# Splitting one Strassen-Winograd product once more, and planning the order anew

## The chip, the cores and the metric

The kernel runs on one core of one Trainium2 chip. The metric is the device time of one execution in microseconds (us), the median of several. TensorE (PE) multiplies matrices, VectorE (DVE), ScalarE (ACT) and GpSimd (POOL) work elementwise, SyncE (SP) issues DMAs.

## The reference

Two parts follow each other. The first is a linear attention with a decaying state (RWKV 5) for batch 4, 8 heads, 768 steps and head size 48:

```python
for t in range(S):
    kt, vt, rt = (k[:, :, t].copy(), v[:, :, t].copy(), r[:, :, t].copy())
    cur = np.einsum('bhd,bhe->bhde', u[None] * kt, vt)
    y[:, :, t] = np.einsum('bhd,bhde->bhe', rt, state + cur)
    state = w[None, :, :, None] * state + np.einsum('bhd,bhe->bhde', kt, vt)
```

Its output, as 3072 tokens of 384 features, goes through a mixture of four experts with hidden size 1024, weighted by the normalised `domain_probs`:

```python
p = domain_probs / (domain_probs.sum(-1, keepdims=True) + 1e-09)
for e in range(E):
    h = np.maximum(x @ w1[e], 0.0)
    out += p[:, e:e + 1] * (h @ w2[e])
```

## The kernel before

The 3072 tokens are 24 chunks of 128 tokens; chunk `ci` is piece `ci // 4` of batch `ci % 4`. Four chunks, one of each batch, make a superchunk; there are six (0 to 5). Each chunk goes through attention: scaling of K and R by powers of the decay (L392, L397), transposes (on PE, or by DMA from chunk 8 on, L442), the products At (L509), a mask (L523, L526), the product Y (L549, L556), the addition of the direct term `dv` (L571) and the new state (L629, L638, L648). GpSimd makes `ruk` and `dv` (L409, L417, L435).

A superchunk then goes through the experts. In superchunks 0 and 1 the second layer is an ordinary product (L738), scaled by the expert's probability on the way out (L749). From superchunk 2 on (`SCALED = 2`) the probability is multiplied in ahead of the first layer (L591), so that the second layer becomes one long product over all four experts: hidden activations of all experts (4096 values of each token, in `hAll`) times `w2` (4096 x 384). First comes the hidden layer of the four experts (`moe`, L707, with the relu L718), 32 groups of three matmuls of 512 columns; then the product stage.

The product stage uses the Strassen-Winograd scheme. For a pair of chunks (`q` = 0 or 1 within the superchunk), A has two block rows (the two chunks) and two block columns (even and odd blocks of 128 hidden values), B = `w2` has two block rows and two block columns of `DH` = 192 output columns. Seven products M1 to M7 replace eight; each is 16 matmuls of 192 columns, in two halves `hf` (experts 0 and 1, experts 2 and 3) of eight matmuls. M1 and M2 are A11 B11 and A12 B21 and meet in the first columns of the first chunk. The sums of A's blocks are made on VectorE (`sum_job`, L874): sum 1 goes into a buffer of its own, sums 3, 2 and 4 are written over blocks of A. The sums of B's blocks are made once (`mix`, L818). M6, M5 and M3 are added onto M1's PSUM region and M4 onto M7's (`ONTO`), each after the copy (ScalarE, L932) or the addition (VectorE, L934) of what stood there before: these are the jobs `C`. The last product of all is M3 of the last pair: its result leaves in two halves, through `o_last` (L927, DMA from SP) and through a ScalarE copy (L929, DMA from ScalarE's queue). The other rows are stored from SP (`store`, L785).

The order of work on each engine is computed when the kernel is built: every piece is a `job` with an estimated duration on each engine, what it needs, a rank, and the buffers that it takes and drops. A list scheduler runs through simulated time, starts on each free engine the ready job with the lowest rank, and the resulting order is issued as it stands. PE's order in the product stage is written out by hand (`SEQ_P`), as is the order of the loads on SP (`ORDER`). `GATES` holds back the scaling of each pair of chunks from chunk 8 on until a given piece of the experts' work is done. After 85 us of simulated time (`LATE`) durations are lengthened: `SLOWER` multiplies those of some engines, and `SHARED` lengthens VectorE's SBUF operations by a share of the time that GpSimd's current operation still takes:

```python
if e == "V" and now > LATE and j.name[0] in ("sum", "scale", "mix", "Xs"):
    us += SHARED * min(us, max(0.0, avail["P"] - now))
```

Of the kernel before, what the change touches and what calls it, by code (L numbers as in the profile page):

```python
# [9 lines left out]
F32 = mybir.dt.float32  # L10
BF16 = mybir.dt.bfloat16
# [3 lines left out]
ALU = mybir.AluOpType  # L15
# [4 lines left out]
def kernel(  # L20
# [12 lines left out]
    nc = tc.nc  # L33

    B, H, S, D = r.shape
    HD = H * D
    C = 128
    NCH = S // C
    TOTC = B * NCH
    SUB = B  # L40
# [81 lines left out]
    for b in range(B):  # L122
# [14 lines left out]

    GATES = [3, 5, 8, 8, 16, 17, 7, 23]  # L140
    WARM, NSPIN = 6.6, 6
    TAIL = {"T": 0.27, "V": 0.17, "A": 0.20, "P": 0.17, "S": 0.0}
    DMAT = 8
# [6 lines left out]
    FIRST = 2  # L150
    SCALED = 2
    ONTO = {6: 1, 5: 6, 3: 5, 4: 7}
    MIX_RANK = 16.0
    XS_ON = {'A': 0.61}
    MIX_ON = {'V': 0.97}
    SCALE_US = 0.97
    VB_ON = {'A': 0.42, 'P': 0.5}
    XS_RANK = 0
    SUM_RANK = -60
    EARLY_SUM = 0.0  # L160
    NSH = 4
    SEQ_S = (((1, 0), (3, 0), (2, 0), (1, 1), (3, 1), (2, 1), (4, 0), (4, 1)),
             ((1, 2), (3, 2), (2, 2), (4, 2)))
    LATE, SLOWER = 85.0, {"V": 1.13, "P": 1.06, "A": 1.15}
    SHARED = 0.6
    SLOTS += [(e, sc, 0) for sc in range(2, SCALED) for e in range(E)]
    ORDER_P = (1, 2, 6, 7, 4, 5, 3)
    SEQ_P = ((0, 1, 0), (0, 2, 0), (0, 7, 0), (0, 1, 1), (0, 2, 1), (0, 7, 1), (0, 6, 0), (0, 6, 1), (0, 4, 0),
# [1 line left out]
             (1, 7, 0), (1, 7, 1), (1, 6, 0), (1, 6, 1), (1, 4, 0), (1, 5, 0), (1, 5, 1), (1, 4, 1), (1, 3, 0),  # L170
             (1, 3, 1))
    EARLY_P = 6
    slots = dict(inp=NIN, wst=NST, RKT=4, AtM=2, Ysb=3, ruk=3, dv=3, Vb=4, At=2, tr=1, ys=1,
                 mm=4, xTe=3, hTs=3, oacc=6, Yse0=1, Yse1=1, Tn=2)
    slots.update({f"{n}{i}": 1 for n, m in (("xTs", 2), ("h", 4), ("S", NSH)) for i in range(m)})
# [6 lines left out]
    def job(name, on, run, needs=(), rank=0.0, takes=(), drops=(), moves=None,  # L182
            behind=()):
        j = Job()
        j.behind = behind
        j.name, j.on, j.run, j.needs, j.rank = name, on, run, list(needs), rank
        j.takes, j.drops, j.moves = takes, drops, moves
        for k in drops:
            tokens[k] = tokens.get(k, 0) + 1
        j.pad = 0.0  # L190
        ci = name[1] if isinstance(name, tuple) and name[0] in ATT else -1
        if ci >= SUB:

            j.pad = PAD_PE if "T" in on else PAD
        j.no = len(jobs)
        assert name not in jobs
        jobs[name] = j
# [61 lines left out]
    def load_p():  # L259
# [1 line left out]
            prow, moe_domain_probs.rearrange("(n p) e -> n p e", p=C)))  # L261

    ORDER = ("K0 K1 R0 R2 R1 V0 K2 w1e0.1 w1e0.0 w1e0.2 V1 K3 V2 R3 w2e0.0 V3 w2e0.1 w2e0.2 p K4 w1e1.1 "
             "w1e1.0 R4 w2e1.0 w1e1.2 K5 R5 w2e1.1 w2e1.2 w1e2.1 V4 w1e2.2 w1e2.0 V5 w2e2.2 V7 K7 w2e2.1 "
             "V6 K6 V8 R6 R7 w2e2.0 w1e3.2 w1e3.1 w1e3.0 K8 V10 K10 w2e3.0 V11 R8 K9 R11 R9 R10 V9 w2e3.2 "
             "K11 V13 w2e3.1 K13 R12 V12 K12 R13 " +
             " ".join(f"c{i}" for i in range(14, TOTC))).split()
    for what in ORDER:
        if what == "p":
            load_p()  # L270
# [93 lines left out]
    def attention(ci):  # L364
# [288 lines left out]
        if c == 0:  # L653
            job(("S", ci), {"V": 0.56}, sv, [("Sm", ci), ("Yout", SUB - 1)], rk + 2, (), (("ys", "S", ci),))
        else:
            job(("Sv", ci), {"V": 0.5}, sv, [("Sm", ci)], rk - 0.1, (("Tn", ci),), (("ys", "S", ci),))
            job(("S", ci), {"P": 1.3}, sp, [("Sv", ci)], rk - 0.5, (), (("Tn", ci),))

    y_sb = weights.tile([128, 3 * HD], BF16)
    y_free, y_at = [0, 1, 2], {}  # L660
# [9 lines left out]
    def h_tag(e, sc):  # L670
        return f"h{3 - e}" if sc >= SCALED else "hTs"
# [170 lines left out]

    s_no, s_last = [0], [None]

    def products(sc, q, at0):
        of = {(m, hf): at0 + n / 7 for n, (x, m, hf) in enumerate(SEQ_P) if x == q}
        c1, c2 = sc * SUB + 2 * q, sc * SUB + 2 * q + 1
        s1, s2 = 2 * q, 2 * q + 1

# [5 lines left out]
        relus = [[("relu", e, sc, fb, 0) for e in (2 * hf, 2 * hf + 1) for fb in range(NFB)]  # L855
                 for hf in range(2)]
        hts = [tuple((h_tag(e, sc), e, sc) for e in (2 * hf, 2 * hf + 1)) for hf in range(2)]
        at_of = {m: of[m, 0] for m in ORDER_P}
        no = s_no[0] % (NSH // 2) * 2
        s_no[0] += 1  # L860
        s_tok = [(f"S{no + hf}", sc, q) for hf in range(2)]
# [5 lines left out]
        def sum_job(k, hf):  # L867
            hs = (0, 1) if hf == 2 else (hf,)

            def run():  # L870
                o, x, y, op = {1: (None, A21, A22, ALU.subtract), 3: (A21, A21, A11, ALU.subtract),
                               2: (A11, None, A11, ALU.subtract), 4: (A12, A12, A11, ALU.add)}[k]
                o, x, y = (s1_of(hf) if z is None else a_of(z, hf) for z in (o, x, y))
                nc.vector.tensor_tensor(o, x, y, op=op)  # L874
            needs = all_cast + [n for h in hs for n in relus[h]]
            if k == 3 and q:
                needs.append(("C", sc, 0, 5))
            if k in (2, 4):
                needs += [("P", sc, q, 1 if k == 2 else 2, h) for h in hs]
            job(("sum", sc, q, k, hf), {"V": 1.23 if hf == 2 else 0.7}, run, needs,  # L880
                at_of[{1: 6, 3: 6, 2: 6, 4: 3}[k]] + (EARLY_SUM if k in (1, 3) and not q and not hf else SUM_RANK), tuple(s_tok[h] for h in hs) if k == 1 else (),
                tuple(x for h in hs for x in hts[h]) + (tuple(s_tok[h] for h in hs) if k in (1, 2) else ()),
                behind=(s_last[0],) if s_last[0] else ())
            s_last[0] = ("sum", sc, q, k, hf)
            for h in hs:
                sum_at[k, h] = s_last[0]
        sum_at = {}
        for k, hf in SEQ_S[q]:
            sum_job(k, hf)
        SUM_OF = {6: 2, 7: 3, 5: 1, 3: 4}  # L890
        def product(m, hf):
# [22 lines left out]
                behind=(p_last[0],) if p_last[0] else ())  # L914
            p_last[0] = ("P", sc, q, m, hf)

        for m in ORDER_P:
            at = at_of[m]

            def c_job(m, s, h, first, drop=()):  # L920
                def run():
                    oacc(c1)
                    o = tl["oacc", c1 // 2][:, s, h * DH:(h + 1) * DH]
                    ps = tl["P", sc, q, m]
                    if m == 3 and c2 == TOTC - 1:
                        rows = out[row0(c1):row0(c1) + C, DH:Dm]
                        nc.vector.tensor_copy(o_last, ps[:, DH // 2:DH])  # L927
                        nc.sync.dma_start(rows[:, DH // 2:DH], o_last)
                        nc.scalar.copy(o[:, 0:DH // 2], ps[:, 0:DH // 2])  # L929
                        nc.scalar.dma_start(rows[:, 0:DH // 2], o[:, 0:DH // 2])  # L930
                    elif first:
                        nc.scalar.copy(o, ps)  # L932
                    else:
                        nc.vector.tensor_add(o, o, ps)  # L934
                needs = [("P", sc, q, m, 1)] + ([] if first else [("C", sc, q, {2: 1, 5: 7, 4: 6}[m])])
                job(("C", sc, q, m), {"A": 0.3} if first else {"V": 0.33}, run, needs, at - 90,
                    (("oacc", c1 // 2),) if m == 1 else (), tuple(("mm", "P", sc, q, x) for x in drop))
            if m == 1:
                c_job(1, 0, 0, True)
            elif m == 2:  # L940
                c_job(2, 0, 0, False, (2,))
                if c2 == TOTC - 1:
                    store(c1, [("C", sc, q, 2)], 0, DH)
            elif m == 6:
                c_job(6, 1, 0, True)
            elif m == 7:
                c_job(7, 1, 1, True)
            elif m == 5:
                c_job(5, 1, 1, False)
            elif m == 4:  # L950
                c_job(4, 1, 0, False, (7,))
                store(c2, [("C", sc, q, 4), ("C", sc, q, 5)])
            else:
                c_job(3, 0, 1, True, (1,))
                if c2 != TOTC - 1:
                    store(c1, [("C", sc, q, 3), ("C", sc, q, 2)])
        return product

    for k, (e, sc, single) in enumerate(SLOTS):
        moe(k, e, sc, single)  # L960
# [22 lines left out]
    for sc in range(SCALED, NSC):  # L983
        at = 8 * (sc - SCALED) + len(SLOTS)
        for e in range(E):
            moe(at + e, e, sc, 0)
        if sc < FIRST:
            for s in range(SUB):
                summed(sc, s, 10.0 + at + 4 + s)
        else:  # L990
            of_pair = [products(sc, q, 10.0 + at + 4) for q in range(2)]
            for q, m, hf in SEQ_P:
                of_pair[q](m, hf)


    left = {j.name: {n for n in j.needs} for j in jobs.values()}
# [33 lines left out]
    events = []  # L1030
    started = []
    gone = set()
    unknown = {n: len(q) for n, q in left.items()}
    known = {n: 0.0 for n in left}
    soon = {e: [] for e in avail}
# [18 lines left out]
    def start(e):  # L1054
# [31 lines left out]
                held.add(t)  # L1086
                free[t[0]] -= 1
        us = j.on[e] * (2.0 if e == "T" and now < WARM and j.name not in ("wmm", "umm") else 1.0)
        if e in SLOWER and now > LATE and j.name[0] not in ("sum", "Xs", "mix", "scale"):
            us *= SLOWER[e]  # L1090
        if e == "V" and now > LATE and j.name[0] in ("sum", "scale", "mix", "Xs"):
            us += SHARED * min(us, max(0.0, avail["P"] - now))
        if j.moves:
            taken, end = dma(now, us, *j.moves)
            us = taken - now + 0.04
        started.append((now, len(started), e, j))
        avail[e] = now + us
        if not j.moves:
            end = now + us + TAIL[e]
        heapq.heappush(events, (avail[e], seq, "eng", e))  # L1100
        heapq.heappush(events, (end, seq + 1, "done", j))
        for u2 in users.get(j.name, ()):
# [8 lines left out]
    while n_done < len(jobs):  # L1111
# [4 lines left out]
            _, _, what, x = heapq.heappop(events)  # L1116
            batch.append((what, x))
        for what, x in batch:
            if what == "done":
                n_done += 1  # L1120
                for t in x.drops:
                    count[t] -= 1
# [63 lines left out]
```

## Time and profile before

| | |
|---|---|
| time, median of 3 runs | 287.18 us (287.02 to 287.48) |
| profiled execution, first to last instruction (span) | 285.2 us |
| time of the profiled execution outside its span | not given by the page; the median is 2.0 us over the span |
| PE busy | 279.3 us, 2677 matmuls |
| VectorE / ScalarE / GpSimd busy | 179.8 / 186.5 / 105.1 us |
| granted TensorE clock | 1.000 |
| DMA, mean | 149 GB/s |

Rows of the profile name a line of the kernel, the engine, the operation, what it writes and reads, the shape, and how often. A matmul's end is modelled, so a matmul's duration is no measure of the rate; the spacing of starts is. The column "idle before" tells what ended the engine's wait. The chain of waits is followed back from the last instruction.

### The profile page before, as it was taken

The numbers are of one execution on the slowest core, as the hardware profiler recorded it, in microseconds if no ns is written. First come the engines' busy times: TensorE is split into PE (matmuls) and PEld (weight loads), VectorE is DVE, ScalarE is ACT, GpSimd is POOL, SyncE is SP. The second block draws the span as 40 slices with busy tenths as digits, with TensorE's granted clock in tenths as the row PEclk, the third lists the DMA queues.
The fourth block names the chain that finished last, engine by engine and source line by source line (L and its number), as shares of the span: only waits on it lengthen the run. The fifth ranks groups of instructions, "written<-read, shape, count | busy, mean of one in ns | idle before, by whom it ended". The sixth has DMA issues, their size and how long they took to land.

```text
span 285.2 us, 6681 instructions
## 1 busy us (share of the span) xinstructions
PE 279.3 (98%) x2677; PEld 193.1 (68%) x2677; DVE 179.8 (63%) x289; ACT 186.5 (65%) x344; POOL 105.1 (37%) x126
## 2 busy tenths in 40 slices
PE   8989999999999999999999999999999999999995
PEld 3777555965774656445899545899644799444995
DVE  5867976679649675998687547798433473010761
ACT  3776868754747485788657788853699850899110
POOL 2883343662796655026157253667010000000000
PEclk9999999999999999999999999999999999999999
DMA  7999999899994988895474996798821241100011
GB/s 152 281 249 339 250 317 268 221 275 238 229 169 91 172 191 143 212 198 118 81 142 116 185 202 118 90 186 129 136 56 28 57 99 42 57 0 0 2 69 44
DMA packets 130290, 42.43 MB, mean 149 GB/s; under 512 B 118458, under 2 KB 130236, under 8 KB 130260
## 3 DMA queue, kind: packets, MB, share of 16 engines
q1 hardware_dynamic: 130100, 41.96, 67.6%
q8 instruction: 21, 0.34, 0.5%
q14 instruction: 9, 0.07, 0.1%
q10 hardware_dynamic: 160, 0.05, 0.1%
HBM read 26.79 MB, written 4.72 MB: 110 GB/s over the span
## 4 chain that ended last, share of the span: by engine, by line
PE 89%; DVE 3%; SPq 3%; DMA 3%; issue 1%; POOL 0%; ACT 0%; DVEq 0%; ACTq 0%
PE hT_ps L707 36%; PE M_ps L905 25%; PE out_ps L738 15%; PE hT_ps L701 5%; DMA RKin<-in_k_dram 3%; SPq L232 2%; PE Y_ps L556 1%; PE At_all L509 1%; PE St_ps L629 1%; PE Y_ps L549 1%; DVE RK_sb L397 1%; PE RKT_ps L461 1%; DVE AtM L523 1%; SPq L246 1%; PE At_ps L509 1%
## 5 line engine op out<-in xcount | busy, mean ns | idle before, releaser
L718 ACT ACTIVATE hAll<-hT_ps 128x512 bf16<-128x512 f32 x168 | 98.7, 597 | 22.5 <-PE hT_ps L707 16.6
L707 PE MATMUL hT_ps<-stg,w_sb 128*128 128x512 bf16 x384 | 85.9, 379 | 0.0
L707 PEld LDWEIGHTS <-w_sb 128*128 128x128 bf16 x504 | 47.2, 98 | 52.2 <-DVE w_sb L80 0.3
L905 PEld LDWEIGHTS <-hAll 128*128 128x128 bf16 x768 | 63.1, 98 | 0.9 <-DVE hAll L874 0.3
L738 PE MATMUL out_ps<-w_sb,hAll 128*128 128x384 bf16 x256 | 45.9, 326 | 0.0
L409 POOL TENSOR_TENSOR ruk<-RKin 128x384 f32<-128x384 f32 x24 | 25.7, 1072 | 50.6 <-DMA RKin<-in_k_dram 31.2
L591 ACT ACTIVATE stg<-dv,p_nat 128x384 bf16<-128x384 f32 x64 | 36.3, 608 | 5.7 <-DMA stg<-stg 5.4
L905 PE MATMUL M_ps<-w_sb,hAll 128*128 128x192 bf16 x384 | 35.3, 246 | 0.0
L932 ACT COPY o_sb<-M_ps 128x192 f32<-128x192 f32 x31 | 9.8, 316 | 37.9 <-PE M_ps L905 37.0
L738 PEld LDWEIGHTS <-hAll 128*128 128x128 bf16 x256 | 23.9, 98 | 15.0
L435 POOL TENSOR_TENSOR dv<-Vt,dcoef 128x384 f32<-128x384 f32 x24 | 21.7, 907 | 27.3 <-ACT stg L591 24.5
L707 PE MATMUL hT_ps<-xTe,w_sb 128*128 128x512 bf16 x120 | 29.2, 379 | 0.0
L417 POOL TENSOR_TENSOR ruk<-ruk,U_sd 128x384 f32<-128x384 f32 x23 | 26.3, 1143 | 1.3
L648 POOL TENSOR_TENSOR S<-Tn,wC 64x192 bf16<-64x192 f32 x32 | 21.6, 674 | 8.2 <-DVE Tn L638 5.1
L874 DVE TENSOR_TENSOR hAll<-stg,hAll 128x1024 bf16<-128x1024 bf16 (+1 forms) x12 | 11.2, 933 | 20.0 <-PE M_ps L905 19.4
L749 DVE SCALAR_TENSOR_TENSOR o_sb<-out_ps,p_nat,o_sb 128x384 f32<-128x384 f32 x24 | 14.7, 616 | 14.0 <-PE out_ps L738 13.3
L874 DVE TENSOR_TENSOR hAll<-hAll 128x1024 bf16<-128x1024 bf16 (+1 forms) x24 | 22.6, 956 | 0.2
L874 DVE TENSOR_TENSOR stg<-hAll 128x1024 bf16<-128x1024 bf16 (+1 forms) x12 | 11.6, 963 | 11.9 <-ACT hAll L718 11.9
L701 PE MATMUL hT_ps<-xTe,w_sb 128*128 128x128 bf16 x288 | 18.7, 219 | 0.0
L934 DVE TENSOR_TENSOR o_sb<-o_sb,M_ps 128x192 f32<-128x192 f32 x24 | 8.4, 351 | 16.3 <-issue 10.3
L905 PE MATMUL M_ps<-w_mix,hAll 128*128 128x192 bf16 x192 | 18.6, 246 | 0.0
L526 DVE TENSOR_TENSOR AtM<-At_all,mask 128x1024 bf16<-128x1024 f32 x8 | 9.7, 1218 | 13.5 <-PE At_all L509 13.5
(89 smaller groups left out, 322.3 us busy)
## 6 DMA issues: line engine op xcount, KB each, us to landing
stg<-in_moe_w_dram SPq DMA_DIRECT2D x16, 576.0 KB, 6.4
RKin<-in_k_dram SPq DMA_DIRECT2D x24, 192.0 KB, 4.3
RKin<-in_r_dram SPq DMA_DIRECT2D x24, 192.0 KB, 3.7
Vt<-in_v_dram SPq DMA_DIRECT2D x24, 192.0 KB, 4.6
out_dram<-o_sb SPq DMA_DIRECT2D x23, 192.0 KB, 2.0
stg<-in_moe_w_dram SPq DMA_DIRECT2D x8, 384.0 KB, 6.4
stg<-stg SPq DMA_TRANSPOSE x32, 2.8
RKT<-RK_sb SPq DMA_TRANSPOSE x16, 3.7
```

The source lines that it names most:

```text
L409: nc.gpsimd.tensor_mul(tl["ruk", ci], tl["Rt", ci], tl["Kt", ci])
L417: nc.gpsimd.tensor_mul(tl["ruk", ci], tl["ruk", ci], U_sd)
L435: nc.gpsimd.tensor_mul(tl["dv", ci], tl["Vt", ci], tl["dcoef", ci].to_broadcast((128, H, D)))
L591: nc.scalar.mul(o, tl["Ysb", ci], p_nat[:, e, n_p:n_p + 1])
L648: nc.gpsimd.tensor_mul(S_new[pr, :, cl], Tn2[pr, tn_at[ci], :, cl], wC[pr, :, None].to_broadcast((P2, NP, D)))
L701: nc.tensor.matmul(ps[:, i, :], w1_sb[:, e, db, (fb + i) * 128:(fb + i + 1) * 128], xTe[:, db, s0, :], start=(i == 0 and db == 0), stop=(i ...
L707: nc.tensor.matmul(ps[:, 0:n, :].rearrange("p a b -> p (a b)"), w1_sb[:, e, db, fb * 128:(fb + 1) * 128], xTe[:, x0 + db, s0:s0 + n, :].re ...
L718: nc.scalar.activation(hTs[:, fb, s0:s0 + n, :], ps[:, 0:n, :], AF.Relu)
L738: nc.tensor.matmul(ps, relu_tile(e, sc)[:, fb, s, :], w2_sb[:, e, fb, :], start=(fb == 0), stop=(fb == NFB - 1))
L749: nc.vector.scalar_tensor_tensor(oacc(ci), in0=tl["o", e, ci], scalar=pe, in1=oacc(ci), op0=ALU.mult, op1=ALU.add)
L874: nc.vector.tensor_tensor(o, x, y, op=op)
L905: nc.tensor.matmul(tl["P", sc, q, m], st, moving(m, hf, n), start=(hf == 0 and n == 0 and m not in ONTO), stop=(hf == 1 and n == 7), skip_ ...
```

## The change

In superchunks 4 and 5 the product M2 is taken out of the seven of each pair. The blocks A12 of both pairs are laid on top of each other and treated as one product, (two block rows: pair 0 and pair 1) x (two block columns) times B21, itself cut into two block rows and two block columns of `DQ` = 96. This product is made with seven products of 96 columns, eight matmuls each (`level2`, jobs `P2`). Its sums of A blocks are the jobs `sum2` (four sums, each in two halves of 512 elements per partition), its sums of B blocks the jobs `mix2` (made once, after the last chunk's attention, in buffers of the K/R loads), and its results are added onto the output rows by jobs `D`, 96 columns at a time. The sums use the `RKT` buffers of attention, the results the PSUM regions `tr` and `ys`. In these superchunks M3's sum (sum 4) also waits for what reads A12 there, all sums of the first level are made in halves, their strict order (`behind`) is dropped, and the PE order is written out as `SEQ_4` and `SEQ_5`; M3 of pair 0 stands next to last there.

The planner now lets a GpSimd operation and a VectorE operation of the kinds in `ONE_PORT` lengthen each other while they overlap; `C` and `D` count as done 0.15 us sooner. The gates, several ranks and the order of the loads after w2e1.2 are others.

```diff
-    GATES = [3, 5, 8, 8, 16, 17, 7, 23]
+    GATES = [4, 3, 8, 8, 15, 11, 20, 18]
...
-    MIX_RANK = 16.0
+    MIX_RANK = 28.0
...
-    XS_RANK = 0
-    SUM_RANK = -60
+    XS_RANK = 2.75
+    SUM_RANK = -50.75
...
-    LATE, SLOWER = 85.0, {"V": 1.13, "P": 1.06, "A": 1.15}
-    SHARED = 0.6
+    LATE, SLOWER = 85.0, {"V": 1.13, "A": 1.15}
+    SHARED = {"V": 0.4, "P": 0.5}
...
+    SEQ_S2 = tuple((k, hf) for k in (1, 3, 2, 4) for hf in range(2))
+    SEQ_4 = ((0, 1, 0), (0, 7, 0), (1, 1, 0), (0, 1, 1), (1, 7, 0), (1, 1, 1), (0, 7, 1), (0, 6, 0), (2, 2, 1),
+             (0, 6, 1), (1, 7, 1), (2, 2, 2), (1, 6, 0), (0, 4, 0), (1, 4, 0), (0, 4, 1), (2, 2, 7), (2, 2, 6),
+             (0, 5, 0), (1, 6, 1), (2, 2, 4), (0, 5, 1), (1, 5, 0), (1, 5, 1), (1, 4, 1), (2, 2, 5), (0, 3, 0),
+             (0, 3, 1), (2, 2, 3), (1, 3, 0), (1, 3, 1))
+    SEQ_5 = ((0, 1, 0), (1, 1, 0), (0, 7, 0), (0, 1, 1), (2, 2, 2), (1, 1, 1), (0, 6, 0), (0, 6, 1), (1, 7, 0),
+             (2, 2, 1), (0, 7, 1), (2, 2, 7), (0, 5, 0), (0, 5, 1), (1, 6, 0), (2, 2, 4), (0, 4, 0), (1, 6, 1),
+             (0, 4, 1), (1, 7, 1), (2, 2, 6), (0, 3, 0), (1, 5, 0), (1, 5, 1), (1, 4, 0), (2, 2, 5), (1, 3, 0),
+             (1, 4, 1), (2, 2, 3), (0, 3, 1), (1, 3, 1))
...
-             "w1e1.0 R4 w2e1.0 w1e1.2 K5 R5 w2e1.1 w2e1.2 w1e2.1 V4 w1e2.2 w1e2.0 V5 w2e2.2 V7 K7 w2e2.1 "
-             "V6 K6 V8 R6 R7 w2e2.0 w1e3.2 w1e3.1 w1e3.0 K8 V10 K10 w2e3.0 V11 R8 K9 R11 R9 R10 V9 w2e3.2 "
-             "K11 V13 w2e3.1 K13 R12 V12 K12 R13 " +
-             " ".join(f"c{i}" for i in range(14, TOTC))).split()
+             "w1e1.0 R4 w2e1.0 w1e1.2 K5 R5 w2e1.1 w2e1.2 V4 w1e2.1 V8 w1e2.2 w1e2.0 V5 w1e3.1 V6 R7 K6 "
+             "V11 K7 K10 w2e2.0 w2e2.1 K9 w2e2.2 R6 R15 V7 w1e3.2 w1e3.0 w2e3.2 K11 R9 R8 R13 R11 K8 V12 "
+             "V13 w2e3.0 V9 w2e3.1 R12 K14 V10 K17 R17 K15 R14 V17 V15 V14 R18 R16 K13 K16 R10 V16 K12 "
+             "K18 V18 " +
+             " ".join(f"c{i}" for i in range(19, TOTC))).split()
...
             if k in (2, 4):
-                needs += [("P", sc, q, 1 if k == 2 else 2, h) for h in hs]
+                if k == 4 and 2 in two:
+                    needs += [("P2", sc, 2, x) for x in (1, 2, 4)] + [("sum2", sc, 2, x, h) for x in (1, 2, 3, 4) for h in hs]
+                else:
+                    needs += [("P", sc, q, 1 if k == 2 else 2, h) for h in hs]
...
+                    for n in range(8):
...
+                        nc.tensor.matmul(o, st[:, 2 * (3 - n // 2) + n % 2, :], mv,
+                                         start=(x in (1, 2) and n == 0), stop=(n == 7), skip_group_check=True)
...
+                if x in (6, 5, 3, 4):
+                    needs.append(("D", sc, m, {6: 1, 5: 6, 3: 5, 4: 7}[x]))
...
+                    nc.vector.tensor_add(o, o, ps)
...
+        if now > LATE and (e == "P" or e == "V" and j.name[0] in ONE_PORT):
+            o = "V" if e == "P" else "P"
+            if avail[o] > now + 1e-9 and (o == "P" or on_port[o].name[0] in ONE_PORT):
+                both = min(us / (1 - SHARED[e]), (avail[o] - now) / (1 - SHARED[o]))
+                us += SHARED[e] * both
+                more = SHARED[o] * both
+                on_port[o].late += more
+                avail[o] += more
...
-            end = now + us + TAIL[e]
+            end = now + us + TAIL[e] - (0.15 if j.name[0] in ("C", "D") else 0.0)
```

## The prediction

> **What bounds the kernel now.** I read the page's shares first, then the chain of waits, then a table by stage, and last the rows of TensorE and VectorE in order of time. The page:
>
> ```profile
> span 285.2 us, 6681 instructions
> PE 279.3 (98%) x2677; PEld 193.1 (68%) x2677; DVE 179.8 (63%) x289; ACT 186.5 (65%) x344; POOL 105.1 (37%) x126
> PE 89%; DVE 3%; SPq 3%; DMA 3%; issue 1%; POOL 0%; ACT 0%; DVEq 0%; ACTq 0%
> ```
>
> PE is busy for 98% and holds 89% of the chain; the rest of the chain is nearly all in the first 20 us (loads) and the last 3 us. But a matmul's end is modelled, so "busy" hides gaps. What counts is the spacing of starts, and the chain in order of time gives it:
>
> ```profile
> 23.71 0.20 PE Y_ps L556 x8
> 25.05 0.17 PE St_ps L629 x4
> 48.95 0.17 PE Y_ps L549 x4
> 224.30 18.48 PE M_ps L905 x224
> 242.78 20.72 PE hT_ps L707 x96
> 263.50 18.50 PE M_ps L905 x224
> 282.02 0.27 DVE o_last L927
> ```
>
> A product matmul of 192 columns starts every 18.48/224 = 82.5 ns, one of 512 columns every 20.72/96 = 216 ns, one of 96 columns (St_ps, Y_ps L549, new weights each) every 0.17/4 = 42.5 ns, one of 48 columns every 25 ns. The last 58 us are three blocks without a gap: product stage of superchunk 4, hidden layer of 5, product stage of 5. After those only copy and store remain.
>
> Where are the gaps? I compared each start with the one before plus its spacing. After 22 us there are four beyond the short regular ones around the At matmuls: 0.37 us at 92.1, 0.28 at 141.7, 0.20 at 151.4, 0.11 at 188.4, together 0.96 us. Two of them in PE's rows:
>
> ```profile
> 89.10 2.75 PE L707 MATMUL hT_ps<-xTe,w_sb 128*128 128x512 bf16 x12
> 92.06 0.33 PE L549 MATMUL Y_ps<-S,RKT 128*128 128x96 bf16 x4 [0.21 <-DVE dv L571]
> 140.14 1.48 PE L905 MATMUL M_ps<-w_sb,hAll 128*128 128x192 bf16 x16
> 141.74 1.49 PE L905 MATMUL M_ps<-o_sb,hAll 128*128 128x192 bf16 x16
> ```
>
> 89.10 + 12 x 0.216 = 91.69, the next start is 92.06; 140.14 + 16 x 0.0825 = 141.46, the next is 141.74. VectorE explains both:
>
> ```profile
> 88.42 3.12 DVE L397 TENSOR_TENSOR RK_sb<-RKin,W_both 128x768 bf16<-128x768 f32 x2
> 199.83 0.95 DVE L397 TENSOR_TENSOR RK_sb<-RKin,W_both 128x768 bf16<-128x768 f32 x1
> 139.63 1.32 DVE L874 TENSOR_TENSOR stg<-hAll 128x1024 bf16<-128x1024 bf16 x1
> 264.80 0.68 DVE L874 TENSOR_TENSOR stg<-hAll 128x1024 bf16<-128x1024 bf16 x1
> ```
>
> The same scale takes 0.95 or 1.56 us, the same sum 0.68 or 1.32, the long ones while GpSimd works. So the kernel is PE's work laid end to end, with under 1 us of holes. It can gain by less PE work or fewer holes; it can lose wherever another engine opens one.
>
> **The change part by part.**
>
> PE. Per superchunk M2 goes: 2 pairs x 2 halves x 8 = 32 matmuls of 192 columns, 32 x 82.5 ns = 2.64 us. In come 7 x 8 = 56 of 96 columns, 56 x 42.5 ns = 2.38 us. That is 0.26 us less, twice: -0.52 us, all on the path. A rule of the Trainium skill speaks against it: TensorE: Matmul & The Clock Gate, "Back-to-back issue gap", says that a sustained stream of weight load and matmul runs at about 81 ns per matmul at 128 columns, since the load has its share. If that held at 96 columns, the 112 new matmuls would cost 9.1 us against 5.28 removed, +3.8. The rows above say otherwise: 42.5 ns with new weights each time, even 25 ns at 48 columns. I take 42.5; the bursts seen are of four to eight, the new ones of eight.
>
> VectorE, per superchunk. Added: eight second-level sums of 512 elements. The half sums (1024) take 0.69 and the full ones (2048) 1.22, so 0.43 each by the slope, 3.4 us. Seven additions of 96 columns from PSUM: between the copy of 128x96 (0.257) and the addition of 128x192 (0.351), I take 0.26, 1.8 us. The second pair's four full sums (4.9 us) become eight half sums (5.5). Removed: two additions of 192 columns, 0.7 us. Net +5.1 us. In superchunk 4 come four weight mixes of 768 elements, between 0.69 (1024) and 0.95 (1536) by the same slope 0.56 each, +2.2 us. In all +12.4 us on VectorE. It costs nothing if hidden under PE, and there is room:
>
> ```profile
> 202.00:224.00 22.00, 22.00 (x148) 10.65 (x146) 5.83 (x9) 20.91 (x40) 0.83 (x1) 1.00 0.39 69
> 224.00:242.70 18.70, 18.70 (x227) 18.58 (x226) 10.37 (x16) 7.32 (x17) 0.00 (x0) 1.00 0.34 75
> 242.70:263.40 20.70, 20.70 (x98) 9.39 (x97) 1.38 (x2) 18.74 (x32) 0.00 (x0) 1.00 0.06 20
> 263.40:285.20 21.80, 18.58 (x225) 18.35 (x223) 10.63 (x17) 3.15 (x10) 0.00 (x0) 1.00 0.11 38
> ```
>
> (After the length: PE, PEld, DVE, ACT, POOL.) The product stages rise from 10.4 to 17.7 and from 10.6 to 15.7 us of VectorE, under 18.2 us of PE. The hidden layers before them leave it 16 and 19 us idle, and in their second half sums of experts 0 and 1 can go there, since the strict order of the sums (`behind`) is dropped: 4 x 0.69 + 4 x 0.43 = 4.5 us. GpSimd is silent in these stages, so they run at the short durations.
>
> Added waits. Products 1, 6, 5, 3 share one PSUM region, as do 2 (its own half), 7, 4; each waits for the addition of the one before. In the written order these lie two or more products apart (0.7 us or more) against about 0.3 for an addition; free. Sum 4 of both pairs (it overwrites the half that M2 reads) now waits for second-level products 1, 2, 4 and all second-level sums. In superchunk 5 product 4 ends some 9.3 us into the stage and the first use of sum 4 is at 12.3: 3 us for two sums of 0.69. In superchunk 4 the gap is about the same. Behind a sum 4 that waits too long on VectorE would stand the additions, and behind those PE. I cost it at 0, up to 0.7 (one sum late).
>
> The end. M3 of the last pair stays last. But pair 0's M3 moves next to last, so its 192 KB store is issued about 0.3 us before PE ends, instead of some ten products earlier, just ahead of the 48 KB store of `o_last` on SP. The transfer of the large one took about 0.6 us and begins some 0.6 us after its issue, so it should be past when the last one flows: 0 to +0.4, I take +0.05.
>
> The new plan. Loads from w1e2.1 on come in another order. Expert 2's second weights stand behind about 0.8 MB more, 3 us at the 263 GB/s of 50 to 60 us; the last was issued at 62 and the products of that time that could use it begin at 77, so cover is about 7 us; without it PE would wait. The K/R loads of several chunks move with it on SP. Gates move the scales (0.95 to 1.56 us each on VectorE) and with them their transposes (1.25 us each on SP), masks and GpSimd's work; the mixes (rank 16 to 28) go behind attention, with 13 us of slack (the last ended at 125.9, the products begin at 138). The first 30 us are fixed by the unchanged head of the load order. Nothing in PE's work changes, so the plan is worth only holes: at best -0.96, at worst new ones. The planner now charges both engines for standing beside each other. Trainium skill, SBUF — State Buffer, "SBUF: two separate sides": VectorE and GpSimd take the shared port for a whole instruction and the other blocks fully. A sum meeting an instruction of 1.1 us could then take 0.69 + 1.1 = 1.8; the rows show 1.32 at most for this size, near the 1.67-fold (1.15) of the new charge, so I trust the plan rather than fear +0.6 per meeting. The four gaps are mostly of this kind, and I take a third to a half of them: -0.35, bounds -0.9 and +1.2.
>
> **Sum.** -0.52 - 0.35 + 0.05 = -0.8 us on the profiled execution's 285.2 us span, 284.4. About 2.0 us lie around the span up to the median of 287.18 and are not touched: 286.4.
>
> **The rivals.**
>
> A. The split alone counts: the plan removes as many holes as it opens. 287.18 - 0.52 = 286.7. For: only 0.96 us of holes were there. Against: two of them have exactly the cause that the new charge models.
>
> B. Slower: VectorE sets the product stages. In superchunk 4, sums, second-level sums, additions and mixes add up to 11.0 + 3.4 + 1.4 + 1.8 + 2.2 = 19.8 us, over PE's 18.2. If the first-half sums do not go ahead of the stage, PE waits 1.6 us there and about 0.3 in superchunk 5: +1.9 - 0.5, 288.6. It decides when less than 1.6 us of VectorE's work goes ahead. Against: some 8 us of idle time in the half stage before it, and before too the first two sums ran at 214, ahead of the stage.
>
> C. The weight loads bound the short matmuls (81 ns): 287.18 + 3.8 = 291.0. Against: St_ps and Y_ps rows.
>
> That the split would not take place can be excluded: both written orders contain the seven products, and M2 leaves the list of first-level products.
>
> **Numbers.** The forecast has 0.50 (own range 285.8 to 286.6), A 0.33 (286.4 to 287.4), B or another hole of over a microsecond 0.15, C 0.02. About 0.2% (0.57 us, bound 286.6) is what measurement can tell from no change. Faster: 0.50 and a quarter of A, 0.58; slower 0.15; same 0.27. The range 285.7 to 287.9 leaves out the best case and most of B and C.
>
> **What would show it.** 112 matmuls of 128x96 in the product stages at 42.5 ns spacing and 832 of 192 columns left, each of the last two product stages 18.2 us in the chain; VectorE near 17 us in them without PE waiting; no gap at 92 and 142. Wrong if the new matmuls are spaced wider than 47 ns (the gain gone: 2.64/56), if PE waits for DVE L874's successor in the last stages, or if a gap over 0.5 us opens between 30 and 200 us.

## The result and the profile after

The changed kernel takes 285.60 us (median of 10 runs, 284.45 to 286.16), the kernel before beside it 286.96; the ratio is 0.9938, with a 95% interval of 0.9918 to 0.9958. The ratio is formed over all the runs and makes 1.8 us less (0.62%, between 0.42 and 0.82%); the two medians differ by 1.36 us. The forecast was 0.8 us: right in sign, but by the ratio more than twice as large. The median lies 0.1 us below the range of 285.7 to 287.9, which started from 287.18 for the kernel before. That kernel gave 286.96 this time, so the miss of the range is no larger than what its median moved; the miss in size is the one to explain.

The page of the changed kernel:

```profile
span 283.9 us, 6814 instructions
PE 277.8 (98%) x2725; PEld 192.7 (68%) x2725; DVE 188.4 (66%) x326; ACT 189.4 (67%) x347; POOL 105.3 (37%) x124
PE 92%; SPq 3%; DMA 3%; DVE 1%; POOL 0%; issue 0%; ACT 0%; ACTq 0%
```

The profiled execution took 285.68 us, 1.8 more than its span. VectorE's share of the chain is down from 3% to 1%: where the chain ran through VectorE at 86 to 92 us (masks, two scales and an addition) and at 139 to 142 us (three sums), it now runs through PE. The chain in order of time, in the last stages:

```profile
223.55 5.28 PE M_ps L924 x64
228.83 0.34 PE M_two L1081 x8
229.17 1.32 PE M_ps L924 x16
...
241.77 20.72 PE hT_ps L719 x96
262.49 2.64 PE M_ps L924 x32
265.13 0.34 PE M_two L1081 x8
...
279.39 1.33 PE M_ps L924 x16
280.75 0.27 DVE o_last L953
```

Eight short matmuls take 0.34 us, 42.5 ns each, as St_ps and Y_ps did. The product stages last 241.77 - 223.55 = 18.22 and 280.75 - 262.49 = 18.26 us, against 18.48 and 282.02 - 263.50 = 18.52: twice 0.26 us less. And the gaps: comparing starts as in the prediction, not one of over 0.07 us is left after 22 us beyond the regular ones around the At and p_ps matmuls. At the places of the two that the prediction showed, PE's rows now run on:

```profile
88.68 2.10 PE L719 MATMUL hT_ps<-xTe,w_sb 128*128 128x512 bf16 x9
90.62 0.33 PE L561 MATMUL Y_ps<-S,RKT 128*128 128x96 bf16 x4
...
140.00 1.48 PE L924 MATMUL M_ps<-w_sb,hAll 128*128 128x192 bf16 x16
141.32 1.48 PE L924 MATMUL M_ps<-o_sb,hAll 128*128 128x192 bf16 x16
```

(88.68 + 9 x 0.216 = 90.62; 140.00 + 16 x 0.0825 = 141.32.)

Because the first 20 us vary by a microsecond with the arrival of the loads, I compare kernels from here on by the *stretch* in the profiled execution: from the first of the four small p_ps matmuls, at 25 to 27 us, to the start of the copy `o_last`. Before it is 282.02 - 25.64 = 256.38 us, after 280.75 - 25.87 = 254.88: 1.50 us less, which is 0.52 of split and 0.96 of gaps to 0.02 us. A stretch is one execution. The span of every run is on record too, so where a kernel ran often the mean of its spans is given beside it: 285.26 us for the kernel before (44 runs beside the first experiments), 283.53 for the changed one (10 runs), 1.73 less. The time outside the span is 1.91 and 1.79 us on average.

VectorE by form, and the stages (after the length the busy time of PE, PEld, DVE, ACT, POOL):

```profile
L1109 DVE TENSOR_TENSOR o_sb<-o_sb,M_two 128x96 f32<-128x96 f32 x14 | 3.5, 251 | 3.4 <-PE M_two L1081 3.1
L1041 DVE TENSOR_TENSOR S_two<-hAll 128x512 bf16<-128x512 bf16 x8 | 3.3, 418 | 12.1 <-ACT hAll L730 12.1
L1008 DVE TENSOR_TENSOR w_two<-w_sb 128x768 bf16<-128x768 bf16 x2 | 1.1, 551 | 0.0
```

```profile
223.55:241.77 18.22, 18.22 (x250) 18.16 (x248) 13.54 (x31) 8.82 (x20) 0.00 (x0) 1.00 0.48 93
241.77:262.49 20.72, 20.72 (x99) 9.45 (x97) 3.84 (x8) 18.83 (x32) 0.00 (x0) 1.00 0.05 18
262.49:283.90 21.41, 18.22 (x249) 17.99 (x246) 12.01 (x28) 3.07 (x9) 0.00 (x0) 1.00 0.12 38
```

The new operations have the forecast durations (0.25, 0.42, 0.55 us against 0.26, 0.43, 0.56). VectorE is busy for 13.5 and 12.0 us of the product stages, less than the 17.7 and 15.7 forecast. Part of its work went ahead of the stages: in the hidden layer of superchunk 5 it now works 3.8 us instead of 1.4. And its whole work rose by 8.6 us (179.8 to 188.4), not by 12.4; where the rest went was not taken apart.

### The profile page after: what moved, and what is told of

Read it like the earlier page. It is cut to its first block, busy times and chain, and to the rows that moved or that the text cites. A ratio compares the mean times of both kernels' runs of the same rounds, so it can differ in the third digit from the quotient of the medians.

```text
span 283.9 us, 6814 instructions
## 1 busy us (share of the span) xinstructions
PE 277.8 (98%) x2725; PEld 192.7 (68%) x2725; DVE 188.4 (66%) x326; ACT 189.4 (67%) x347; POOL 105.3 (37%) x124
## 4 chain that ended last, share of the span: by engine, by line
PE 92%; SPq 3%; DMA 3%; DVE 1%; POOL 0%; issue 0%; ACT 0%; ACTq 0%
PE hT_ps L719 39%; PE M_ps L924 24%; PE out_ps L750 15%; PE hT_ps L713 5%; DMA RKin<-in_k_dram 3%; SPq L243 2%; PE M_two L1081 2%; PE At_all L521 2%; PE Y_ps L568 1%; PE St_ps L641 1%; PE Y_ps L561 1%; PE RKT_ps L473 1%; PE At_ps L521 1%; SPq L257 1%; POOL RK_sb L404 0%; PE xT_ps L625 0%
## 5 line engine op out<-in xcount | busy, mean ns | idle before, releaser
L719 PEld LDWEIGHTS <-w_sb 128*128 128x128 bf16 x504 | 47.0, 98 | 51.4 <-DVE w_sb L80 0.3
L924 PEld LDWEIGHTS <-hAll 128*128 128x128 bf16 x704 | 57.9, 98 | 0.9
L603 ACT ACTIVATE stg<-dv,p_nat 128x384 bf16<-128x384 f32 x64 | 36.6, 609 | 6.3 <-DMA stg<-stg 6.3
L447 POOL TENSOR_TENSOR dv<-Vt,dcoef 128x384 f32<-128x384 f32 x24 | 23.3, 974 | 45.4 <-ACT stg L603 37.0
L750 PEld LDWEIGHTS <-hAll 128*128 128x128 bf16 x256 | 23.7, 98 | 15.2
L924 PE MATMUL M_ps<-w_sb,hAll 128*128 128x192 bf16 x320 | 30.2, 246 | 0.0
L660 POOL TENSOR_TENSOR S<-Tn,wC 64x192 bf16<-64x192 f32 x32 | 21.0, 655 | 18.0 <-DVE Tn L650 16.7
L761 DVE SCALAR_TENSOR_TENSOR o_sb<-out_ps,p_nat,o_sb 128x384 f32<-128x384 f32 x24 | 14.8, 617 | 15.7 <-PE out_ps L750 15.5
L924 PE MATMUL M_ps<-o_sb,hAll 128*128 128x192 bf16 x192 | 18.6, 246 | 0.0
L713 PEld LDWEIGHTS <-w_sb 128*128 128x128 bf16 x288 | 16.7, 98 | 0.6
L442 DVE TENSOR_REDUCE dcoef<-ruk 128x8 f32<-128x384 f32 x24 | 13.0, 545 | 6.1 <-POOL ruk L429 5.9
```

The costliest lines, as they stand in the source:

```text
L447: nc.gpsimd.tensor_mul(tl["dv", ci], tl["Vt", ci], tl["dcoef", ci].to_broadcast((128, H, D)))
L603: nc.scalar.mul(o, tl["Ysb", ci], p_nat[:, e, n_p:n_p + 1])
L660: nc.gpsimd.tensor_mul(S_new[pr, :, cl], Tn2[pr, tn_at[ci], :, cl], wC[pr, :, None].to_broadcast((P2, NP, D)))
L713: nc.tensor.matmul(ps[:, i, :], w1_sb[:, e, db, (fb + i) * 128:(fb + i + 1) * 128], xTe[:, db, s0, :], start=(i == 0 and db == 0), stop=(i ...
L719: nc.tensor.matmul(ps[:, 0:n, :].rearrange("p a b -> p (a b)"), w1_sb[:, e, db, fb * 128:(fb + 1) * 128], xTe[:, x0 + db, s0:s0 + n, :].re ...
L750: nc.tensor.matmul(ps, relu_tile(e, sc)[:, fb, s, :], w2_sb[:, e, fb, :], start=(fb == 0), stop=(fb == NFB - 1))
```

## The experiments

The theory: the split is worth its 0.52 us, the rest is gaps that the new plan closed. What was open is which part of the plan closed them, and how. In the changed source each part can be set back by itself; with all set back, the rows of VectorE, ScalarE and GpSimd come in the order of the kernel before.

**Without the split, and the split alone.**

```diff
-    SEQ_OF = {4: SEQ_4, 5: SEQ_5}
+    SEQ_OF = {}
```

> The changed kernel without the split (SEQ_OF = {}): M2 is made as before in all superchunks, with the new planner, gates, ranks and loads. Theory 1 (the split is worth its 0.52 us of PE work, the new plan closed all 0.96 us of gaps): the last two product stages take 18.5 us again, no gap over 0.1 us after 22 us, from the first At_all after the first load to the last product 262.65 us, the time about 0.5 us over the changed kernel. Rival (the gaps went because the split freed PSUM buffers or moved VectorE's work): gaps come back, 263.2 us or more, the time 1 us or more over the changed kernel.

Measured: 286.17 us, ratio to before 0.9969 (0.9957 to 0.9981); no gaps; stretch 255.40 us, 0.52 more than the changed kernel. So in the stretch the split is worth its PE work, and the gaps close without it. The mean span of the 22 runs is 284.30 us, 0.96 (give or take 0.3) under the kernel before: that is what the plan by itself is worth.

The split alone: the gates, ranks and loads set back, and with them the planner's durations (the edits of this diff and of the one further down, both at once):

```diff
-    GATES = [4, 3, 8, 8, 15, 11, 20, 18]
+    GATES = [3, 5, 8, 8, 16, 17, 7, 23]
...
-    MIX_RANK = 28.0
+    MIX_RANK = 16.0
...
-    XS_RANK = 2.75
-    SUM_RANK = -50.75
+    XS_RANK = 0
+    SUM_RANK = -60
...
-             "w1e1.0 R4 w2e1.0 w1e1.2 K5 R5 w2e1.1 w2e1.2 V4 w1e2.1 V8 w1e2.2 w1e2.0 V5 w1e3.1 V6 R7 K6 "
+             "w1e1.0 R4 w2e1.0 w1e1.2 K5 R5 w2e1.1 w2e1.2 w1e2.1 V4 w1e2.2 w1e2.0 V5 w2e2.2 V7 K7 w2e2.1 "
...
```

> The changed kernel with the old gates, ranks, loads and the old planner's durations: only the split and its order are left. Theory 1: product stages of 18.2 us, the four gaps at 92, 142, 151 and 188 us still there (0.9 to 1.0 us in all), 263.1 us from the first At_all to the last product, 0.5 us under the kernel before and 1.0 us over the changed one. Rival (the plan has no part in it): gaps gone, within 0.2 us of the changed kernel.

Measured: ratio 0.9983 (0.9961 to 1.0004); gaps of 0.25 us at 91 and 0.27 at 141, stretch 255.46. Those at 151 and 188 us were absent, although VectorE, ScalarE and GpSimd have the order of the kernel before up to 216 us: small gaps vary between executions. Of the 0.9 to 1.0 us of gaps that were expected this execution had 0.52. The ratio understates this run: its span (mean of 14 runs 284.52) is 0.74 us under that of the kernel before, but the time outside the span is 2.36 us instead of 1.91. What adds 0.45 us there was not followed up. (The 0.62 us gap of this execution at 24.6 us belongs to the loads: PE waits for a cast of expert weights. It lies ahead of the stretch.)

**Which part of the plan.** First the new gates, ranks and loads with the old durations, as in this diff; then the old gates, ranks and loads (the diff above) with the new durations:

```diff
-    LATE, SLOWER = 85.0, {"V": 1.13, "A": 1.15}
-    SHARED = {"V": 0.4, "P": 0.5}
+    LATE, SLOWER = 85.0, {"V": 1.13, "P": 1.06, "A": 1.15}
+    SHARED = 0.6
...
+        if e == "V" and now > LATE and j.name[0] in ONE_PORT + ("Xs",):
+            us += SHARED * min(us, max(0.0, avail["P"] - now))
...
-            end = now + us + TAIL[e] - (0.15 if j.name[0] in ("C", "D") else 0.0)
+            end = now + us + TAIL[e]
...
-            job(("S", ci), {"P": 1.3 if ci < 2 * SUB else 1.1}, sp, [("Sv", ci)], rk - 0.5, (), (("Tn", ci),))
+            job(("S", ci), {"P": 1.3}, sp, [("Sv", ci)], rk - 0.5, (), (("Tn", ci),))
```

> The changed kernel with its new gates, ranks and loads, but with the planner's old durations (no mutual lengthening, C and D done at the old time, the old GpSimd factor). Theory 2 (the new charge for VectorE beside GpSimd closed the gaps): two or more gaps over 0.1 us come back, 0.4 us or more in all. Theory 3 (the gates, ranks and loads closed them): gaps of under 0.3 us in all, time within 0.3 us of the changed kernel.

> The changed kernel with the new planner, but the old gates, ranks and load order. Theory 2 (the charge closed the gaps): under 0.3 us of gaps, time within 0.3 us of the changed kernel. Theory 3 (gates, ranks and loads): 0.6 us of gaps or more, time 0.5 us or more over it.

Measured: with the old durations, ratio 0.9961 (0.9947 to 0.9975), the gap at 140 us is there (0.27), that at 92 is not, stretch 255.16. With the new durations and the old gates, ratio 0.9950 (0.9931 to 0.9968), no gap at all, stretch 254.88, the changed kernel's to the hundredth. The mean spans are 284.05 and 283.67 us. So with the old gates, ranks and loads the new durations suffice; the gates, ranks and loads close the gap at 92 by themselves but not the one at 141. The two are no sum: they are two ways to close the same gaps.

The durations were then taken apart, with the old gates, ranks and loads: only the mutual lengthening (the last two places above set back: the earlier end of `C` and `D` and the states' shorter duration), and only the earlier end of `C` and `D`. In the second run the states' duration was set back too, other than its expectation says.

> The kernel of the old gates, ranks and loads with the split, and of the new durations only the mutual lengthening of VectorE and GpSimd (C, D and the states' duration as before). If the mutual lengthening closed the gaps that the run with the split alone had at 91 and 141 us (0.25 and 0.27 us), both are gone here and the stretch from the p_ps matmuls to the last product is 254.9 to 255.1 us (against 255.46 there); if it was the earlier end of C and D, both are there still.

> The counterpart: old gates, ranks and loads, old lengthening, with C and D counted as done 0.15 us sooner and the states' shorter duration. If the mutual lengthening closed the gaps, those at 91 and 141 us stay (0.4 to 0.6 us in all, 255.4 us from the p_ps matmuls to the last product); if it was C and D, they are gone.

With the lengthening alone both gaps went, as expected, but two others came, 0.55 us at 196.6 and 0.37 at 199.0 (stretch 255.80; ratio 1.0000, 0.9977 to 1.0023): my figure for the stretch was missed. Without the lengthening both stayed, 0.40 and 0.27, with 0.33 at 188.1 and 0.15 at 197.7 besides (stretch 256.03, also more than the 255.4 expected). So the lengthening is what closes these two, but alone it gains nothing (mean span 285.04, against 284.52 of the split alone). Together with the other two new durations, as in the run of the old gates, the later gaps do not open. By their rows the two at 197 to 199 end on jobs `C`, a copy on ScalarE and an addition on VectorE, the kind whose end the new durations put earlier. Whether that removes them, or the states' shorter duration, was not tested.

What the lengthening does at 88 us shows in VectorE's rows of the run with the new durations and old gates:

```profile
88.40 1.51 DVE L408 TENSOR_TENSOR RK_sb<-RKin,W_both 128x768 bf16<-128x768 f32 x1
89.83 0.55 DVE L582 TENSOR_TENSOR dv<-Y_ps,dv 128x384 f32<-128x384 f32 x1
90.30 1.28 DVE L408 TENSOR_TENSOR RK_sb<-RKin,W_both 128x768 bf16<-128x768 f32 x1
```

The scales are as slow as before, but the addition that PE's next Y waits for stands between them instead of behind both. In the changed kernel no scale stands there: VectorE's rows have one at 84.57 and the next only after 93 us. The cure is order, not speed.

**How VectorE and GpSimd stand beside each other.** GpSimd's row of the kernel before at the second gap:

```profile
139.17 1.24 POOL L435 TENSOR_TENSOR dv<-Vt,dcoef 128x384 f32<-128x384 f32 x1 [4.89 <-ACT stg L591]
```

VectorE's rows there are this sum, and right behind it the one of 1.32 us at 139.63 that the prediction shows:

```profile
139.03 0.69 DVE L874 TENSOR_TENSOR hAll<-stg,hAll 128x1024 bf16<-128x1024 bf16 x1 [1.96 <-PE M_ps L905]
```

GpSimd's `dv` takes 0.83 alone; here it ends at 140.41, 0.69 after the first sum. The second sum ends at 139.63 + 1.32 = 140.95, 0.54 after GpSimd. I compared ends for all overlapping pairs of a GpSimd operation with a sum or scale of VectorE (two inputs from SBUF) in this trace after 85 us: where GpSimd was first, a sum of 1024 ends 0.55 us after it, a sum of 2048 1.08, a scale 0.81 to 0.82, whatever the overlap; where VectorE was first, `dv` ends 0.69 after it, `ruk` 0.86, the states 0.36. Of 33 pairs 30 keep these distances to within about 10 ns; the other three are 0.02 to 0.10 us longer. VectorE's additions from PSUM keep no distance from the same GpSimd operations (where GpSimd was first, they end between 0.60 us before it and 0.30 after it). So a sum or scale and a GpSimd operation do not run at once: the second waits for the end of the first, and then takes its own time less some 0.14 us (the sum takes 0.69 alone, `dv` 0.83, `ruk` 1.00, the states 0.50). In the changed kernel GpSimd and VectorE have these rows:

```profile
138.56 1.05 POOL L447 TENSOR_TENSOR dv<-Vt,dcoef 128x384 f32<-128x384 f32 x1 [4.31 <-ACT stg L603]
```

```profile
138.24 0.69 DVE L889 TENSOR_TENSOR hAll<-stg,hAll 128x1024 bf16<-128x1024 bf16 x1 [1.69 <-PE M_ps L924]
139.51 0.69 DVE L889 TENSOR_TENSOR stg<-hAll 128x1024 bf16<-128x1024 bf16 x1 [0.59 <-ACT hAll L730]
140.24 0.69 DVE L889 TENSOR_TENSOR hAll<-hAll 128x1024 bf16<-128x1024 bf16 x1
```

Here PE makes the first product of the stage 0.8 us earlier (at 137.38 instead of 138.17), the first sum follows it, and `dv` comes behind that; `dv` ends at 139.61, just after the second sum begins. To test it by hand I took the order of before and changed two places: `put_behind` moves a job behind another in the finished list, here the second of the two scales behind the addition that PE waits for at 92 us (chunk 8's), and the probe, a copy of one column, makes GpSimd wait for the third sum:

```diff
+    put_behind(("scale", 11, 0), ("Yout", 8))
...
+    probe.run = lambda: nc.gpsimd.tensor_copy(scratch, hAll[:, 0, 1, 0:1])   # ahead of dv 15
```

> The kernel before, its order untouched but for two places: on VectorE the scale of chunk 11 comes behind the addition of chunk 8 (L571 of before) instead of ahead of it, and GpSimd first copies one column that the second sum at 140 us writes, so that its dv of chunk 15 cannot run among the three sums at 139 to 141 us. If whole-instruction blocking at the shared port made these two gaps, both are gone, the sum that took 1.32 us takes 0.69, and from the p_ps matmuls to the last product it is 255.75 us (256.38 before). If VectorE and GpSimd only slow each other and something else held PE, the gap at 141 us stays.

GpSimd and VectorE of this run:

```profile
141.70 0.70 POOL L1321 COPY scratch<-hAll 128x1 bf16<-128x1 bf16 x1 [6.01 <-DVE hAll L888]
142.36 0.82 POOL L446 TENSOR_TENSOR dv<-Vt,dcoef 128x384 f32<-128x384 f32 x1
```

```profile
139.54 0.69 DVE L888 TENSOR_TENSOR hAll<-stg,hAll 128x1024 bf16<-128x1024 bf16 x1 [1.96 <-PE M_ps L923]
140.15 0.68 DVE L888 TENSOR_TENSOR stg<-hAll 128x1024 bf16<-128x1024 bf16 x1
140.87 0.69 DVE L888 TENSOR_TENSOR hAll<-hAll 128x1024 bf16<-128x1024 bf16 x1
```

With `dv` held back, the second sum takes 0.68 us and PE's next product starts at 141.98 without a gap (16 matmuls from 140.66 end there). At the other place the addition for PE's Y now stands between the scales, and PE goes on at once (89.99 + 12 x 0.216 = 92.58):

```profile
89.99 2.75 PE L718 MATMUL hT_ps<-xTe,w_sb 128*128 128x512 bf16 x12
92.58 0.33 PE L560 MATMUL Y_ps<-S,RKT 128*128 128x96 bf16 x4
```

Both gaps are gone; the stretch is 255.87, with gaps of 0.26 at 188.7 and 0.22 at 198.4. The time of this single run (287.63) says nothing at this size. The control:

> The kernel before with its order, as a control: the changed source with the split, the new durations, gates, ranks and loads all set back. Gaps at 92 and 141 us of 0.25 to 0.4 us each if they belong to the order, 256.0 to 256.5 us from the p_ps matmuls to the last product; those at 151 and 188 us may be of one execution only.

Gaps of 0.21 at 93, 0.27 at 143, 0.20 at 152, 0.45 at 190 and 0.47 at 200, together 1.60 us; stretch 257.03. The first of them, in PE's and VectorE's rows (90.27 + 12 x 0.216 = 92.86, the next start is 93.07):

```profile
90.27 2.75 PE L718 MATMUL hT_ps<-xTe,w_sb 128*128 128x512 bf16 x12
93.07 0.33 PE L560 MATMUL Y_ps<-S,RKT 128*128 128x96 bf16 x4
89.58 2.97 DVE L408 TENSOR_TENSOR RK_sb<-RKin,W_both 128x768 bf16<-128x768 f32 x2
92.47 0.55 DVE L582 TENSOR_TENSOR dv<-Y_ps,dv 128x384 f32<-128x384 f32 x1
```

So the gap at the start of the products is in every run with the old durations and the order unmoved (five of five), and the one at 92 in every run with the old order there (four of four, 0.21 to 0.40 us). Moving two places removed both, though in one execution. Those at 188 to 200 us come and go. And the old order loses 0.96 us in one execution and 1.60 in another.

> The changed kernel once more: if its closed gaps belong to the order, none of over 0.1 us after the p_ps matmuls, and 254.8 to 255.0 us from them to the last product. A gap in one execution alone, as the run with doubled sums had one at 87 us, would show how much an execution varies.

No gap over 0.1 us in the stretch, which is 254.85. The new order holds in these two: 254.88 and 254.85 against 256.38 and 257.03. The next run shows that it does not do so always.

**VectorE's room.** Every second-level sum twice, the order untouched:

```diff
-                    nc.vector.tensor_tensor(S[k][:, half], x[:, half], y[:, half], op=op)
+                    for _ in range(2):
+                        nc.vector.tensor_tensor(S[k][:, half], x[:, half], y[:, half], op=op)
```

> The changed kernel with each second-level sum made twice, the order otherwise untouched: 3.4 us more of VectorE's work by isolated durations (2.8 us back to back) in each of the last two superchunks. If VectorE has the room that the forecast counted on (product stages of 18.2 us, VectorE filled up to about 17 us), PE waits for under 0.3 us in each stage. If VectorE is near its limit (rival B), each product stage grows by 1 us or more.

In superchunk 4 PE waits once for 0.12 us, in superchunk 5 not at all: there is room for about 3 us more. The stretch, 255.44, contains a gap of 0.41 us at 87.4, where the order is that of the changed kernel. A load came later here, GpSimd's `ruk` with it (83.80 to 84.80), and the scale that began at 83.89 took 1.72 us instead of 0.95: it ended 0.81 after `ruk`, the distance of above. PE waited for the masks behind it. This is the only one of the five executions with this order that has the gap. Then the cover taken away:

```diff
-            needs = all_cast + [n for h in hs for n in relus[h]]
+            needs = all_cast + [n for h in ((0, 1) if two else hs) for n in relus[h]]
```

and the same for the second-level sums, with `EARLY_SUM = -52.0`.

> The changed kernel planned so that no sum of the last two superchunks begins before the last relu of its hidden layer (the first two sums get the rank of the others). Rival B put the price of losing that cover at 1.6 us in superchunk 4 and 0.3 us in superchunk 5. If that working is right the stages become 19.8 and 18.5 us; if the written PE order needs the early sums, since its third product already waits for one, they become 20 us or more each.

Superchunk 5's stage takes 286.73 - 266.52 = 20.2 us, with one wait of 1.94 us ahead of the product at 273.3; rival B's working had 0.3. It compared totals, but the written order asks for many of the sums in the first third of the stage, so the wait is set by when each is due. In superchunk 4 the wait is 2.86 us by the starts, against 1.6 in rival B's working. The chain puts its end down to ScalarE's scaling L603, but the weight load of that product waits for VectorE, which works on sums without a pause from 223.91 on and ends one at 228.34, 0.05 us before the load:

```profile
228.39 0.61 PEld L924 LDWEIGHTS <-hAll 128*128 128x128 bf16 x5 [2.92 <-DVE hAll L889]
```

So both waits are waits for sums. The single run took 291.99 us.

This run also has the gap at the start of superchunk 2's products again, 0.27 us at 140.8, although it was planned with the new durations. `dv` meets the second sum as in the kernel before, and the sum ends 0.55 us after it:

```profile
138.42 1.05 POOL L447 TENSOR_TENSOR dv<-Vt,dcoef 128x384 f32<-128x384 f32 x1 [4.79 <-ACT stg L603]
138.70 1.32 DVE L889 TENSOR_TENSOR stg<-hAll 128x1024 bf16<-128x1024 bf16 x1
```

The mutual lengthening therefore does not rule such a meeting out; it made plans without one in the changed kernel and in the run with the old gates.

**One split more.** M4 of superchunk 5 split as well. M4's part of superchunk 5 is not computed as the reference has it in this kernel, so it is read for its time alone.

```diff
-    SEQ_5 = ((0, 1, 0), (1, 1, 0), (0, 7, 0), (0, 1, 1), (2, 2, 2), (1, 1, 1), (0, 6, 0), (0, 6, 1), (1, 7, 0),
...
+    SEQ_5 = ((0, 1, 0), (1, 1, 0), (0, 1, 1), (2, 4, 2), (1, 1, 1), (0, 7, 0), (1, 7, 0), (0, 7, 1), (0, 6, 1),
...
```

> The changed kernel with M4 of superchunk 5 split as M2 is (its product stage then has 14 short products; an order for them found with the planner). PE's work falls by another 0.26 us, VectorE's rises by about 7 us there (eight more sums, seven more additions, four more mixes, less nothing). If VectorE's room is what limits such splits, PE waits 0.3 us or more in that stage and nothing is won: stage of 18.2 us or more, time equal to the changed kernel or up to 0.5 us slower. If room is left, the stage takes 18.0 us.

Ratio 0.9938 (0.9914 to 0.9962), the changed kernel's. The stage takes 280.69 - 262.52 = 18.17 us: of another 0.26 us of PE work about 0.1 arrives, since PE waits 0.17 us at 275.15 for the addition of the short product before (that ends at 275.09). With this order nothing that can be measured is left in that direction; no version here beats the changed kernel.

## Why the prediction was right and wrong

*The split, -0.52 us: right.* Stages of 18.2 us, spacing 42.5 ns, stretch 0.52 longer without it. The figure of about 81 ns per matmul at 128 columns (Trainium skill, TensorE: Matmul & The Clock Gate, "Back-to-back issue gap"), taken for 96 columns, would have made it a loss of 3.8 us, by estimate; the rows of short matmuls in the trace decided rightly against it.

*VectorE's work at no cost: right,* with every duration within about 0.01 us; twice the second-level sums cost 0.12 us. (The slack of the mixes is 138 - 125.9 = 12 us, not 13; nothing hangs on it.)

*The end, +0.05 us: right in being nothing.* From `o_last` to the end of the span it is 3.15 us before and after.

*The plan, -0.35 us: this step failed.* It was worth -0.96 by the mean spans of the run without the split, -0.96 against the profiled execution of before and -1.60 against the second. Two things were wrong in it. First, "I take a third to a half" was a discount without a reason in the profile: the four gaps had all been found, and the two at 92 and 141 were no chance but faults of the order, there in every execution of it. Second, I read the durations (1.32 against 0.68) as a slowing by a factor and set the rule of the exclusive port (Trainium skill, SBUF — State Buffer, "SBUF: two separate sides") aside. The ends of the two engines' rows would have shown that it holds here, to within about 10 ns in 30 of 33 pairs: 1.32 us is the rest of `dv`, 140.41 - 139.63 = 0.78, and then 0.54. The 1.8 us that the prediction missed in the rows would need both to start at once. With blocking the loss depends on which of two instructions starts first (`ruk` 0.09 us ahead of the scale, in the run with doubled sums), so an order that keeps them apart closes such a gap wholly, not by a third; that the planner finds one is likely, not certain, as the run with the late sums shows. And I took one execution's sum of gaps as the bound of what they can be; where gaps hang on such races, that bound moves.

*The sum.* With the step at its measured size, -0.52 - 0.96 (to -1.60) + 0 = -1.5 to -2.1 us, which holds the measured -1.8. By the means it is -1.73 in the span and -0.12 outside it; that last part the prediction had at nothing, and what makes it is open.

*Rival A,* the split alone, would be a ratio of 0.998, and that is what the run with the split alone gave (0.9983), in part by luck, as 0.45 us more outside the span hid a span that was 0.74 us shorter. It was not the case for the changed kernel, because the plan did its part. *Rival B* did not come, and its price was set too low. *Rival C* is excluded by the spacing.

## What to carry to other kernels

When an engine is full end to end, list every hole of its rows by starts, and ask of each whether it is a fault of the order or a chance; a fault of the order can be closed wholly, and should be counted so once the new order is seen to avoid it. To see how two engines disturb each other, compare their ends, not their durations: a constant distance of ends is a lock, and a lock is cured by the order of two instructions. Look at a second execution before a sum of small gaps is taken as a bound.

## What the hardware showed besides

VectorE's operations with two SBUF inputs and GpSimd's wait for each other by whole instructions (distance of ends 0.55, 1.08 and 0.81 us for three shapes, as above). And the longest gap had a second price. In the run with the late sums PE was idle for 2.69 us in superchunk 4, by its rows:

```profile
224.22 1.48 PE L924 MATMUL M_ps<-w_sb,hAll 128*128 128x192 bf16 x16
228.40 1.46 PE L924 MATMUL M_ps<-o_sb,hAll 128*128 128x192 bf16 x8 [2.69 <-ACT stg L603]
229.65 1.49 PE L924 MATMUL M_ps<-w_sb,hAll 128*128 128x192 bf16 x8
```

```profile
223.00:245.80 22.80, 20.11 (x250) 19.63 (x249) 14.22 (x33) 8.89 (x20) 0.00 (x0) 0.93 0.38 72
266.52:289.90 23.38, 18.39 (x248) 17.94 (x246) 14.55 (x34) 3.06 (x9) 0.00 (x0) 1.00 0.11 35
```

The next eight matmuls take 229.65 - 228.40 = 1.25 us instead of 0.66, the starts lie 0.16 us apart until 231.9, and the granted clock of the stage is 0.93: about 1.8 us more are lost after the wait (4.46 us in the chain for 32 matmuls that take 2.64). The wait of 1.94 us in superchunk 5 left the clock at 1.00. Each was seen once, so where between them it turns is open.
